# The first block of z in halves on two engines each, and the third turn moved into the tile of a pair of banks

## Chip, cores, metric

One NeuronCore of a Trainium2 chip. The metric is the device time of one execution in microseconds, taken on the slowest core, which here is the only one. The kernel before took 1192.81 us (median of three runs, 1192.8 to 1194.91). The whole change lies in the first 13 us of the program.

## The reference

```python
# batch 8, seq S 3008, d_model 256, d_qk 64, d_ff 2048; fp32 in and out
scores = (1.0 / S) * np.matmul(z, z.transpose(0, 2, 1))
attn = np.maximum(scores, 0.0) ** 2
x = u * np.matmul(attn, v)                    # [8, 3008, 256]
h = x.reshape(-1, 256) @ w_in                 # [24064, 2048]
y = (h * np.cos(h)) @ w_out                   # [24064, 256]
```

## The kernel before

It works on blocks of 512 rows of z. At the start each block of the first batch is loaded as f32, cast to f16, turned on TensorE (four transposes of 128x128) and copied from PSUM to `zT`. From `zT` come the scores, in groups of 128x1024 over two PSUM banks. Each group passes through a relu into a tile `r` and a square into a tile `A`, and `A` is multiplied with v (the "products" below). The program order on each engine is the order of this code. Waits between engines are put in by the framework, tile by tile.

```python
turned = [ppool.tile([P, CW], FP16, name=f"turned{i}", tag=f"M{i % 2}") for i in range(3)]
turned_e = ppool.tile([P, 2, 2 * CW], FP16, name="turned_e", tag="E2")     # two banks
turned += [turned_e[:, 0, 0:CW], turned_e[:, 1, 0:CW], turned_e[:, 0, CW:2 * CW]]
...
def emit_score(later=None):
    ...                                       # two or four matmuls into e, 128x1024 f32
    r = rpool.tile([P, 2, CW], FP16, name="r")
    nc.scalar.activation(r[:, :, 0:W], e[:, :, 0:W], AF.Relu)
    def square(): ...                         # nc.vector.tensor_tensor(a4, r, r, ALU.mult)
    if later is None:
        square()
    else:
        later.append(square)
...
def copy_turned(g):
    dst = zTs[0][:, g * CW:(g + 1) * CW]
    if g == 0:
        nc.scalar.copy(dst, turned[g])
    else:
        nc.vector.tensor_copy(dst, turned[g])
...
for i in range(7):                            # warm-up
    nc.tensor.matmul(E[i % 2][:, 0, :], warm[:, 0:P], warm, start=True, stop=True)
cast_z(nc.vector, 0)
cast_z(nc.vector, 1)
cast_z(nc.vector, 2)
for g in range(3, NC):
    cast_z(nc.gpsimd, g)
    ...
squares = []
turn_on_pe(0)
copy_turned(0)
turn_on_pe(1)
copy_turned(1)
emit_score(later=squares)
emit_score(later=squares)
turn_on_pe(2)
copy_turned(2)                                # third copy, ahead of the squares
squares.pop(0)()
squares.pop(0)()
M = [ppool.tile([P, CW], FP32, name=f"M{i}", tag=f"M{i}") for i in range(2)]

def filler(n):                                # matmuls whose result nobody reads
    for i in range(n):
        nc.tensor.matmul(M[1], warm[:, 0:P], warm, start=True, stop=True)

turn_on_pe(3)
copy_turned(3)
filler(2)
emit_score()
filler(1)
emit_score()
filler(1)
...
phase_a_first(0, 12, {4: lambda: turn_late(4), 8: lambda: turn_late(5)})   # products; fifth, sixth turn
```

In the text turns, copies, scores, relus and squares are counted from one: the third turn is `turn_on_pe(2)`.

## Time and profile before

| | kernel before |
|---|---|
| median of three runs | 1192.81 us |
| span of the profiled execution | 1191.2 us |
| TensorE busy, and its share of the chain that ended last | 99%, 98% |
| first score starts | 5.46 us |
| third score, first product, sixth score start | 7.41, 8.75, 12.15 us |

The sixth score is a convenient milestone: from the first products on, both kernels have the same instructions in the same order, so a difference in its start time is the whole effect of the change on the start. The prediction below shows the stretches, the chain and VectorE's order. TensorE's own timeline shows how the turns stand in it (columns: start, busy time, engine, source line, operation, output from inputs, shapes, count, and in brackets the idle time ahead with what ended it):

```profile
6.43 0.40 PE L658 MATMUL turned<-id,z 128*128 128x128 f16 x4
6.66 0.39 PE L658 MATMUL turned_e<-id,z 128*128 128x128 f16 x4
6.88 0.59 PE L696 MATMUL M<-s 128*128 128x512 f16 x2
7.41 0.39 PE L202 MATMUL E<-zT 64*128 64x512 f16 x2
```

The fourth turn (`turned_e`, 6.66) follows the third (`turned`, 6.43) at once, because it has a tile of its own. Two fillers (L696) bridge the time until the third score.

### The profile page before, as it was taken

What the parts mean: (1) busy time and instruction counts of PE and PEld (TensorE: products, weight loads), DVE (VectorE), ACT (ScalarE), POOL (GpSimd) and SP (SyncE); (2) the same over time, 40 slices, a digit from 0 to 9 for tenths busy, and PEclk for the clock granted to TensorE, in tenths of its full rate; (3) what the DMA queues carried; (4) which work ended last, traced back from release to release, by engine and by line L of the source; (5) the groups of instructions that cost most, each with busy time, mean ns of one, the idle gap of its engine ahead of it and who ended that gap; (6) DMA issues with size and microseconds to landing.
All of it is one profiled execution on the core that took longest, in us unless ns stands there. A gap on an engine that the chain in (4) does not pass through costs nothing.

```text
span 1191.2 us, 29044 instructions
## 1 busy us (share of the span) xinstructions
PE 1183.7 (99%) x11887; PEld 726.8 (61%) x11887; DVE 1011.5 (85%) x1302; ACT 794.9 (67%) x927; POOL 679.0 (57%) x717
## 2 busy tenths in 40 slices
PE   9999999999999999999999999999999999999998
PEld 4556665665566656666566665656666566665566
DVE  6888888889988898888988889888888888888776
ACT  7966676667666676667676676666766666666454
POOL 3286745657466573755647556476555655545452
PEclk9999999999999999999999999999999999999999
DMA  9999999569995799955999469984798837974301
GB/s 160 175 172 158 115 171 130 102 122 104 173 127 101 123 137 166 126 89 103 155 152 130 86 106 158 168 123 70 120 162 152 122 72 120 173 122 84 65 20 54
DMA packets 449142, 148.00 MB, mean 124 GB/s; under 512 B 401264, under 2 KB 432496, under 8 KB 449008
## 3 DMA queue, kind: packets, MB, share of 16 engines
q1 hardware_dynamic: 368464, 112.93, 56.6%
q0 software_dynamic: 80032, 32.78, 27.7%
q8 instruction: 93, 1.52, 0.5%
q10 hardware_dynamic: 512, 0.43, 0.1%
q14 instruction: 41, 0.34, 0.1%
HBM read 66.32 MB, written 24.64 MB: 76 GB/s over the span
## 4 chain that ended last, share of the span: by engine, by line
PE 98%; ACT 1%; DVE 1%; issue 0%; POOL 0%; DVEq 0%; ACTq 0%
PE E L412 27%; PE M L490 23%; PE M L266 20%; PE E L266 19%; PE E L202 6%; PE M L533 1%; ACT r L212 1%; PE M L468 1%; DVE g L423 0%; PE E L673 0%; DVE sm L278 0%; PE E L533 0%; POOL s L441 0%; PE M L696 0%; ACT c L420 0%
## 5 line engine op out<-in xcount | busy, mean ns | idle before, releaser
L420 ACT ACTIVATE c<-E 128x1024 f16<-128x1024 f32 (+1 forms) x384 | 385.7, 1007 | 216.4 <-PE E L412 214.1
L423 DVE SCALAR_TENSOR_TENSOR g<-E,c 128x1024 f16<-128x1024 f32 (+1 forms) x384 | 458.9, 1197 | 62.0 <-ACT c L420 60.9
L212 ACT ACTIVATE r<-E 128x512 f16<-128x512 f32 (+1 forms) x342 | 328.0, 967 | 112.3 <-PE E L202 106.6
L266 PEld LDWEIGHTS <-v 64*128 64x128 f16 x4512 | 245.7, 94 | 229.6 <-issue 18.8
L412 PE MATMUL E<-x,w_in 128*128 128x512 f16 (+1 forms) x1408 | 354.0, 375 | 0.0
L441 POOL TENSOR_TENSOR s<-g 128x512 f16<-128x512 f16 (+1 forms) x184 | 207.8, 1130 | 189.3 <-DVE g L423 139.4
L266 PE MATMUL M<-A,v 64*128 64x512 f16 (+1 forms) x2256 | 283.0, 372 | 0.0
L266 PE MATMUL E<-A,v 64*128 64x512 f16 (+1 forms) x2256 | 278.0, 371 | 0.0
L442 POOL TENSOR_TENSOR g<-g 128x512 f16<-128x512 f16 (+1 forms) x184 | 219.0, 1190 | 14.4
L412 PEld LDWEIGHTS <-w_in 128*128 128x128 f16 x1536 | 133.1, 98 | 108.9 <-issue 19.5
L490 PEld LDWEIGHTS <-g 128*128 128x128 f16 x2816 | 172.5, 98 | 40.8
L217 DVE TENSOR_TENSOR A<-r 128x1024 f16<-128x1024 f16 x240 | 173.2, 734 | 15.1 <-ACT r L212 14.3
L294 POOL TENSOR_TENSOR x<-sm,uT 128x512 f16<-128x512 f32 (+1 forms) x43 | 48.6, 1131 | 223.5 <-DVE sm L278 223.5
L490 PEld LDWEIGHTS <-s 128*128 128x128 f16 x2112 | 129.4, 98 | 32.1 <-DVE s L448 0.5
L202 PE MATMUL E<-zT 64*128 64x512 f16 (+4 forms) x684 | 128.0, 356 | 1.6 <-DVE sm L278 0.7
L448 DVE TENSOR_TENSOR s<-s,g 128x1024 f16<-128x1024 f16 (+1 forms) x92 | 99.7, 1085 | 2.1 <-POOL s L441 2.1
L490 PE MATMUL M<-w_mix,s 128*128 128x128 f16 x1408 | 94.0, 219 | 0.3 <-POOL s L441 0.3
L490 PE MATMUL M<-w_mix,g 128*128 128x128 f16 x1408 | 93.6, 219 | 0.0
L490 PE MATMUL M<-w_out,g 128*128 128x128 f16 x1408 | 93.6, 219 | 0.0
L220 DVE TENSOR_TENSOR A<-r 128x512 f16<-128x512 f16 (+1 forms) x102 | 80.1, 785 | 8.6 <-ACT r L212 7.6
L202 PEld LDWEIGHTS <-zT 64*128 64x128 f16 x684 | 38.7, 94 | 38.4 <-issue 3.8
L450 DVE TENSOR_TENSOR s<-g,s 128x1024 f16<-128x1024 f16 (+1 forms) x92 | 60.6, 661 | 0.0
(58 smaller groups left out, 636.3 us busy)
## 6 DMA issues: line engine op xcount, KB each, us to landing
out_dram<-o SPq DMA_DIRECT2D x87, 256.0 KB, 2.1
v<-in_v_dram POOLq DMA_DIRECT2D x40, 256.0 KB, 11.5
u<-in_u_dram POOLq DMA_DIRECT2D x40, 256.0 KB, 4.5
A<-A SPq DMA_TRANSPOSE x252, 5.3
z<-in_z_dram POOLq DMA_DIRECT2D x14, 192.0 KB, 10.9
z<-in_z_dram POOLq DMA_DIRECT2D x14, 176.0 KB, 6.8
v<-in_v_dram POOLq DMA_DIRECT2D x8, 192.0 KB, 16.1
u<-in_u_dram POOLq DMA_DIRECT2D x8, 192.0 KB, 3.7
```

The lines of the kernel that those rows point to most:

```text
L202: nc.tensor.matmul(e[:, t, 0:Wt], zT[rows, k * P:(k + 1) * P], zT[rows, J * CW:J * CW + Wt], start=True, stop=True,)
L212: nc.scalar.activation(r[:, :, 0:W], e[:, :, 0:W], AF.Relu)
L217: nc.vector.tensor_tensor(a4, r4, r4, ALU.mult)
L220: nc.vector.tensor_tensor(a4, r[:, :, 0:W], r[:, :, 0:W], ALU.mult)
L266: nc.tensor.matmul(bank[:, 0:width(J)], vs[b, k // 4][t * H:(t + 1) * H, k % 4, dh * P:(dh + 1) * P], value_rhs(b, J, k, t), start=start, ...
L412: nc.tensor.matmul(e[:, f, 0:W], w_in16[:, k, ft * P:(ft + 1) * P], x[:, k, 0:W], start=(k == 0), stop=(k == 1),)
L420: nc.scalar.activation(c[:, :, 0:W], e[:, :, 0:W], AF.Sin, bias=half_pi, scale=inv_s2)
L423: return lambda: nc.vector.scalar_tensor_tensor(gs[m][:, 2 * i:2 * i + 2, 0:W], e[:, :, 0:W], 1.0, c[:, :, 0:W], ALU.mult, ALU.mult)
L441: nc.gpsimd.tensor_tensor(s1[:, f, 0:n], g[:, f, low], g[:, lower, low], ALU.add)
L442: nc.gpsimd.tensor_tensor(g[:, f, low], g[:, f, up], g[:, f, low], ALU.subtract)
L448: nc.vector.tensor_tensor(s2[:, f, 0:n], s1[:, f, 0:n], g[:, f, up], ALU.subtract)
L490: nc.tensor.matmul(acc[:, k * P:(k + 1) * P], left[:, ft, k * P:(k + 1) * P], right[:, ft, :], start=(ft == 0 and k == 0), stop=(ft == F - ...
```

## The change

Its intent, as far as the code tells it: shorten the way to the first scores by splitting the cast, the copy and the relu of the first block over two engines each; free the bank M0 by moving the third turn into the pair of banks; and start the first two squares before the third copy.

```diff
@@ -73,9 +73,12 @@
     mark = kpool.tile([1, 2], FP16, name="mark")
     z32_all = gpool.tile([P, NC, 4, dqk], FP32, name="z32", tag="g")
     z32 = [z32_all[:, i, :, :] for i in range(NC)]
-    turned = [ppool.tile([P, CW], FP16, name=f"turned{i}", tag=f"M{i % 2}") for i in range(3)]
+    turned = [ppool.tile([P, CW], FP16, name=f"turned{i}", tag=f"M{i}") for i in range(2)]
     turned_e = ppool.tile([P, 2, 2 * CW], FP16, name="turned_e", tag="E2")
-    turned += [turned_e[:, 0, 0:CW], turned_e[:, 1, 0:CW], turned_e[:, 0, CW:2 * CW]]
+    turned += [
+        turned_e[:, 1, 0:CW], turned_e[:, 0, 0:CW],
+        turned_e[:, 1, CW:2 * CW], turned_e[:, 0, CW:2 * CW],
+    ]
     E = [ppool.tile([P, 2, CW], FP32, name=f"E{i}", tag=f"E{i}") for i in range(2)]
 
     ctx.enter_context(tc.manual_schedule())
@@ -187,7 +190,7 @@
     turn_slots = {}
     done_groups = [0]
 
-    def emit_score(later=None):
+    def emit_score(later=None, shared=False):
         b, J, I, h = groups[done_groups[0]]
         done_groups[0] += 1
         cut = I == J and not (b == 0 and J < 3)
@@ -209,7 +212,11 @@
         key = (b, J, I)
         a = new_piece(key) if h == 0 else piece(key)
         r = rpool.tile([P, 2, CW], FP16, name="r")
-        nc.scalar.activation(r[:, :, 0:W], e[:, :, 0:W], AF.Relu)
+        if shared:
+            nc.scalar.activation(r[:, 0, 0:W], e[:, 0, 0:W], AF.Relu)
+            nc.vector.tensor_scalar_max(r[:, 1, 0:W], e[:, 1, 0:W], 0.0)
+        else:
+            nc.scalar.activation(r[:, :, 0:W], e[:, :, 0:W], AF.Relu)
         def square():
             if I > J:
                 a4 = a.rearrange("p (k t j) -> p t k j", k=4, j=P)[:, 2 * h:2 * h + 2, :, :]
@@ -649,21 +656,22 @@
     make_identity(nc, id16)
     load_v(0, 0)
 
-    def cast_z(eng, g):
-        dst = z16s[0][:, 4 * g:4 * g + 4, :].rearrange("p k (t d) -> p k t d", t=2)
-        eng.tensor_copy(dst, z32[g].unsqueeze(2).to_broadcast([P, 4, 2, dqk]))
+    def cast_z(eng, g, lo=0, hi=4):
+        dst = z16s[0][:, 4 * g + lo:4 * g + hi, :].rearrange("p k (t d) -> p k t d", t=2)
+        eng.tensor_copy(dst, z32[g][:, lo:hi, :].unsqueeze(2).to_broadcast([P, hi - lo, 2, dqk]))
 
     def turn_on_pe(g):
         for k in range(4):
             nc.tensor.matmul(
                 turned[g][:, k * P:(k + 1) * P], z16s[0][:, 4 * g + k, :], id16,
-                is_transpose=True, start=(k == 0 and g < 5), stop=(k == 3),
+                is_transpose=True, start=(k == 0 and g < 4), stop=(k == 3),
             )
 
     def copy_turned(g):
         dst = zTs[0][:, g * CW:(g + 1) * CW]
         if g == 0:
-            nc.scalar.copy(dst, turned[g])
+            nc.vector.tensor_copy(dst[:, 0:T], turned[g][:, 0:T])
+            nc.scalar.copy(dst[:, T:CW], turned[g][:, T:CW])
         else:
             nc.vector.tensor_copy(dst, turned[g])
 
@@ -671,22 +679,21 @@
     nc.scalar.activation(wc[:, 0, 0:P], warm[:, 0:P], AF.Sin)
     for i in range(7):
         nc.tensor.matmul(E[i % 2][:, 0, :], warm[:, 0:P], warm, start=True, stop=True)
-    cast_z(nc.vector, 0)
+    cast_z(nc.vector, 0, 0, 2)
+    cast_z(nc.gpsimd, 0, 2, 4)
     cast_z(nc.vector, 1)
+    turn_on_pe(0)
+    copy_turned(0)
     cast_z(nc.vector, 2)
     for g in range(3, NC):
         cast_z(nc.gpsimd, g)
         if g == 3:
             load_v(0, 1)
     squares = []
-    turn_on_pe(0)
-    copy_turned(0)
     turn_on_pe(1)
     copy_turned(1)
+    emit_score(later=squares, shared=True)
     emit_score(later=squares)
-    emit_score(later=squares)
-    turn_on_pe(2)
-    copy_turned(2)
     squares.pop(0)()
     squares.pop(0)()
     M = [ppool.tile([P, CW], FP32, name=f"M{i}", tag=f"M{i}") for i in range(2)]
@@ -695,11 +702,13 @@
         for i in range(n):
             nc.tensor.matmul(M[1], warm[:, 0:P], warm, start=True, stop=True)
 
+    turn_on_pe(2)
+    copy_turned(2)
+    filler(1)
     turn_on_pe(3)
+    emit_score()
     copy_turned(3)
     filler(2)
-    emit_score()
-    filler(1)
     emit_score()
     filler(1)
 
```

## The prediction

> **What bounds it now.** I read the page's busy times first, then the whole chain of waits by line, then a table of stretches, then the chain and the timeline of the first 13 us, because the change touches nothing later than that.
>
> ```profile
> PE 1183.7 (99%) x11887; PEld 726.8 (61%) x11887; DVE 1011.5 (85%) x1302; ACT 794.9 (67%) x927; POOL 679.0 (57%) x717
> ...
> PE 98%; ACT 1%; DVE 1%; issue 0%; POOL 0%; DVEq 0%; ACTq 0%
> ...
> 8.75:12.57 3.82, 3.63 (x33) 1.50 (x34) 2.97 (x7) 2.16 (x3) 3.82 (x6) 1.00 0.62 71
> 12.57:24.00 11.43, 11.43 (x108) 5.95 (x106) 7.92 (x13) 11.42 (x14) 1.95 (x4) 1.00 1.22 194
> ...
> 60.00:1191.00 1131.00, 1126.55 (x11434) 697.61 (x11432) 967.46 (x1236) 743.48 (x870) 661.90 (x688) 1.00 0.84 122
> ```
>
> TensorE is 98% of the chain and busy 1126.55 of the last 1131 us. From 12.57 to 24.00 TensorE and ScalarE are both busy all the time (11.43 and 11.42 of 11.43 us). So nothing behind 12.57 us can take up a shift of the start: whatever the start gains or loses goes to the end one to one. Even a start of no length would save about 1%. The question is therefore one of a few tenths of a us up to two or three.
>
> The start, from the chain in order of time and the timeline:
>
> ```profile
> 4.36 0.44 PE turned L658 x4
> 4.82 0.59 ACT zT L666
> 5.46 1.03 PE E L202 x2
> 6.49 0.33 PE turned L658 x4
> 6.83 0.22 PE turned_e L658 x4
> ...
> 8.82 0.97 PE M L266 x8
> 9.79 0.33 PE turned_e L658 x4
> ...
> 12.15 0.41 PE E L202 x2
> ```
> ```profile
> 3.48 1.10 DVE L654 CAST z<-z 128x512 f16<-128x512 f32 x3 [2.35 <-DMA z<-in_z_dram]
> 6.86 0.42 DVE L668 COPY zT<-turned 128x512 f16<-128x512 f16 x1 [1.19 <-PE turned L658]
> 7.20 1.57 DVE L220 TENSOR_TENSOR A<-r 128x1024 f16<-128x1024 f16 x2
> 8.69 0.42 DVE L668 COPY zT<-turned_e 128x512 f16<-128x512 f16 x1
> 9.03 1.58 DVE L217 TENSOR_TENSOR A<-r 128x1024 f16<-128x1024 f16 x2
> ```
>
> The reader should see the order on VectorE: the third copy (6.86) stands ahead of the first two squares (7.20), and the fourth (8.69) ahead of the third and fourth squares (9.03). TensorE walks through turns, scores, fillers and the first products almost without a gap from 6.43 to 12.15.
>
> **The Trainium skill.** "PSUM — Partial Sum Buffer", PSUM bank collisions raise a hardware error: two engines may not touch one bank (in the same 32 partitions) at once, reads against reads included, so readers have to be kept apart. The trace before agrees only in that no bank there is read by two engines at once; the waits of the changed program show the consequence below. "SBUF — State Buffer", Who interferes with whom: VectorE in a two-port mode, or with two SBUF inputs against a GpSimd instruction that reads SBUF, shuts GpSimd out, or the other way round. The trace agrees in kind: GpSimd's casts took 0.61 us, but the one that met two squares 0.89. "ScalarE: Activation LUTs", What ACT_TABLE_LOAD costs: an ACTIVATE has a fixed part plus 0.833 ns an element; the trace has 1024 elements at 1.02 us and 512 at 0.59, the same slope. "TensorE: Matmul & The Clock Gate", Part 1: an idle window of about 3.4 us halves TensorE's clock. No such case is in this trace after its warm-up (turns start 107 ns apart at 4.15, 56 ns apart from 6.49).
>
> **The change part by part**, with the order and the waits of the built changed program at hand. They are the same as before from the first products on, except for what follows. Costs of halves are estimates from the rows. ScalarE: 1.02 for 1024 and 0.59 for 512, so 0.37 for 256. VectorE: 0.69 for a square of 1024 and 0.42 for a copy of 512, both f16, so 0.29 for 256; a 512-element read of f32 out of PSUM took 0.68 (sm<-M). Signals cost 0.04 to 0.07 us in the records (turn ends 4.784, copy starts 4.821; relu ends 7.138, square starts 7.204).
>
> Cast in halves: the whole cast ran 3.48 to 3.91, but TensorE's seven warm-up matmuls start 0.427 us apart, 3.723 being the last, so the first turn can't start before 4.15, as it did. The faster cast is worth 0. GpSimd's half waits for the same landing (3.456) and takes, as an estimate, 0.4 us; if VectorE's two casts shut it out until 4.1, two of the four turns come at 4.55, some 0.2 late. I count 0.05.
>
> Copy in halves: both halves lie in one bank, and in the built program ScalarE's half waits for VectorE's half, not for the turn. So 4.82 + 0.29 + 0.04 + 0.37 = 5.52, where the whole copy ended at 5.41. Loss 0.11.
>
> Relu in halves: VectorE's half waits for ScalarE's half. ScalarE's runs from 6.11 + 0.11 = 6.22 to 6.82, VectorE's from 6.89 (0.07 for the signal) to 7.57. r is whole at 7.57 in place of 7.14; the first square goes from 7.20 to about 7.62 and ends at 8.31, the second runs to 8.92 (before: 8.78). ScalarE itself is free 0.3 us sooner, for the second relu.
>
> Third turn into the pair of banks, and the new order: this is the large term. The squares now come before the third copy on VectorE, and the third copy runs at about 8.84 to 9.26 in place of 6.86 to 7.29. The fourth turn now shares a tile with the third, and in the built program it waits for the third copy; before it followed the third turn at once, at 6.66. TensorE, in order, has one filler between and then stands from about 7.2 to 9.31. Behind the fourth turn is the third score. A turn and the gap behind it take 0.33 (11.233 to 11.563 in the records), so that score starts at 9.64 in place of 7.41: 2.2 us late.
>
> From there: third relu 10.06 to 11.09 (7.94 to 8.97 before); filler, filler, fourth score, filler, at 0.216 each, and the first eight products from about 10.8 (before 8.75) to 11.7. The fifth turn waits for the fourth copy, which now stands behind the third square: 11.09 + 0.07 + 0.69, then 0.42 less 0.08 of overlap, so 12.19; the turn starts at 12.24 in place of 9.72. TensorE stands another 0.55 us. After it the order is as before: fifth score 0.77 behind that turn, sixth score 2.43 behind it, so 14.67 in place of 12.15.
>
> Sum at the sixth score: +2.5 by this walk. Of it 2.2 is the wait of the fourth turn and 0.3 that of the fifth, the copy's 0.11 and the relu's part being within the first. Before, there were 0.19 us of wait ahead of the sixth score that need not all return, and the walk takes no credit for ScalarE's earlier second relu. I take 2.3. From 12.57 on the order and work are those of before, with TensorE full, so 1192.8 + 2.3 = 1195.1.
>
> **Rivals.** First, the one that the change was made for: casts, copy and relu each in half the time, first score some 0.4 us sooner, third copy not waited for, and 1192.4 or less. For it speaks that the chain runs through the ScalarE copy (0.59) and relu (1.02 each) at the start; against it the waits of the built program, which put the halves one behind the other. Second, the late turns are absorbed: ScalarE gains 0.3 us on the second relu, products could run ahead, and the stretch to 24 us hides the rest; the time stays at 1192.8 to 1193.3. Against it: in 12.57 to 24.00 TensorE is full, 11.43 of 11.43, as is ScalarE, and only 0.19 us of wait stands ahead of 12.15. Third, the two us of standstill let TensorE's clock fall back, and the scores and products from 9.3 to some 13 us run at half speed: about 3 us of TensorE work there would add up to 3 us, giving 1197 to 1198. Against it: the standstill is shorter than the window of that page and has filler work on both sides. Fourth, GpSimd is shut out of its half cast for longer and every step moves by 0.2 to 0.5: 1195.3 to 1195.6.
>
> **Range and chances.** The kernel before ran at 1192.8 twice and 1194.9 once, so single runs scatter by 2 us. The second rival sets the low end, 1193.5, the third the high end, 1197.2. Two per cent is 24 us, as long as the whole start: within 2% is all but certain. I think it slower by some 0.2%, with about one chance in ten that it is not slower at all.
>
> **What would show it.** Right: the half copies of block 0 stand in line (ScalarE's starting about 5.15), likewise the half relus; VectorE's order is copy, half relu, two squares, third copy at about 8.8; a standstill of TensorE of about 2 us before the fourth turn, put down to the copy of zT on VectorE, and a second of about half a us before the fifth; the sixth score near 14.6; from there equal durations, and the span 2 to 2.5 us longer. Wrong: the fourth turn starting before 8.5; the third copy ahead of the squares; TensorE full from 7 to 12 us; or the shift at 14.6 us not found again at the end.

## The result, and the profile after

The changed kernel took 1197.38 us (median of 6 runs, 1196.83 to 1197.96). The kernel before took 1193.18 (6 runs, the three above among them, 1192.8 to 1197.65). The ratio of fast runs is 1.0028 with a 95% interval of 1.0013 to 1.0043: slower, and well within 2%. All runs were fast, that is, none was over 1.5% above the fastest of its kernel. Here and below a ratio is the mean time of one kernel's fast runs over that of the other's fast runs of the same rounds, so it is not quite the ratio of the medians quoted. The profiled spans are 1191.2 and 1195.3, so 4.1 us longer.

The direction was as predicted, and so was the wait. The size was not: 2.3 us were predicted, 4.1 came, because TensorE's clock, which the prediction had put aside, and a held-up square came on top. Against the 1192.81 known at the time, the ratio gives 1196.1, inside the range (the one long execution of before, 1197.65, makes the ratio smaller); the median of the runs lies 0.2 us above its upper end.

The stretches of the changed kernel (columns: stretch and length in us, then busy us and count for PE, PEld (weight loads), DVE, ACT, POOL, then TensorE's granted clock, DMA share, GB/s; a clock of 1.00 is full, 0.50 half. The column shows 1.00 also ahead of the first clock record, here at 6.14 us, although the turns at 4.15 still start 107 ns apart):

```profile
4.15:8.75 4.60, 2.47 (x18) 1.35 (x17) 2.95 (x7) 1.88 (x3) 3.05 (x5) 1.00 1.01 135
8.75:12.57 3.82, 2.91 (x11) 0.76 (x10) 1.55 (x4) 1.20 (x2) 3.82 (x6) 0.60 0.76 90
12.57:16.00 3.43, 3.43 (x29) 1.30 (x29) 1.70 (x5) 1.84 (x2) 1.43 (x3) 0.94 1.32 163
```

From 8.75 to 12.57 TensorE did 11 matmuls where it had done 33, and its clock column fell from 1.00 to 0.60. That column is the surprise. The chain of the changed kernel in order of time (start, length, engine, what):

```profile
4.82 0.30 DVE zT L673
...
5.14 0.38 ACT zT L674
...
6.21 0.60 ACT r L216
...
6.84 0.70 DVE r L217
...
7.57 1.71 DVE A L227 x2
9.28 0.34 DVE zT L676
...
9.66 0.58 PE turned_e L665 x4
10.25 0.54 PE E L205 x2
10.79 0.96 PE M L703 x2
```

The halves stand one behind the other, as predicted: VectorE's half copy, then ScalarE's; ScalarE's half relu, then VectorE's. Then come both squares, the third copy, and only then the fourth turn. The timeline of the same stretch:

```profile
6.37 0.40 PE L665 MATMUL turned_e<-id,z 128*128 128x128 f16 x4
6.60 0.38 PE L703 MATMUL M<-s 128*128 128x512 f16 x1
...
7.57 1.71 DVE L227 TENSOR_TENSOR A<-r 128x1024 f16<-128x1024 f16 x2
7.64 1.09 POOL L661 CAST z<-z 128x512 f16<-128x512 f32 x1 [1.23 <-DMA z<-in_z_dram]
...
9.66 0.58 PE L665 MATMUL turned_e<-id,z 128*128 128x128 f16 x4 [2.69 <-DVE zT L676]
```

Three things are to be seen. TensorE stands idle for 2.69 us ahead of the fourth turn, put down to the copy of `zT` on VectorE. The two squares took 1.71 us: single records give 0.69 for the first (7.57 to 8.26) and 1.10 for the second (8.18 to 9.28), beside a GpSimd cast of 1.09 (7.64 to 8.73). And the four transposes of the fourth turn took 0.58, where the four of the third took 0.40: TensorE is at half clock. In the single records the clock is low from 9.55 to 12.96 us, 3.41 us in all; the stretches agree, (1 - 0.60) x 2 x 3.82 + (1 - 0.94) x 2 x 3.43 being 3.5.

| start, us | before | predicted | after |
|---|---|---|---|
| first score | 5.46 | 5.57 | 5.57 |
| ScalarE's half copy | - | 5.15 | 5.14 |
| VectorE's half relu | - | 6.89 | 6.84 |
| first square | 7.20 | 7.62 | 7.57 |
| third copy | 6.86 | 8.84 | 9.20 |
| fourth turn | 6.66 | 9.31 | 9.66 |
| third score | 7.41 | 9.64 | 10.18 |
| first product | 8.75 | 10.8 | 12.77 |
| fifth turn | 9.72 | 12.24 | 13.81 |
| sixth score | 12.15 | 14.67 | 16.24 |

The sixth score is 4.09 us late, and ScalarE's instructions, matched one by one with those of before, stay 4.01 to 4.10 late from the fifth relu to the end (the span: +4.12). What had to be found out is how the 4.09 splits.

### The profile page after: what moved, and what is told of

The parts are those of the page before. It is cut to its first block, busy times and chain, and to the rows that moved or that the text cites. A ratio compares the mean times of both kernels' runs of the same rounds, so it can differ in the third digit from the quotient of the medians.

```text
span 1195.3 us, 29046 instructions
## 1 busy us (share of the span) xinstructions
PE 1185.0 (99%) x11887; PEld 727.1 (61%) x11887; DVE 1012.5 (85%) x1304; ACT 793.9 (66%) x927; POOL 678.5 (57%) x718
## 4 chain that ended last, share of the span: by engine, by line
PE 97%; DVE 1%; ACT 1%; issue 0%; POOL 0%; DVEq 0%; ACTq 0%
PE E L419 27%; PE M L497 23%; PE M L273 20%; PE E L273 19%; PE E L205 5%; PE M L540 1%; ACT r L219 1%; PE M L475 1%; DVE g L430 0%; PE E L681 0%; DVE A L227 0%; DVE sm L285 0%; PE E L540 0%; PE M L703 0%; PE turned_e L665 0%
## 5 line engine op out<-in xcount | busy, mean ns | idle before, releaser
L219 ACT ACTIVATE r<-E 128x1024 f16<-128x1024 f32 x341 | 327.1, 966 | 116.0 <-PE E L205 110.1
L449 POOL TENSOR_TENSOR g<-g 128x512 f16<-128x512 f16 (+1 forms) x184 | 218.7, 1188 | 14.4
## 6 DMA issues: line engine op xcount, KB each, us to landing
v<-in_v_dram POOLq DMA_DIRECT2D x8, 192.0 KB, 16.2
```

What stands on the lines that cost most here:

```text
L449: nc.gpsimd.tensor_tensor(g[:, f, low], g[:, f, up], g[:, f, low], ALU.subtract)
```

## The experiments

Theory A: the shared tile and the place of the third copy behind both squares make the wait, and the wait alone is worth about 2.4 us; the rest is TensorE's clock. Rival B: the rest is VectorE being held up by GpSimd. Rival C: the halves cost more than their 0.1 us. Rival D: part of the 4.09 is something later, unrelated to the start.

All ten kernels gave correct results. The readings rest on the traces of the start. These agree closely (the first score starts at 5.57 in all nine kernels with the halves) and differ by some tenths of a us where a load of z lands earlier or later. Each median stands beside that of the kernel before on the same chip in the last columns. "Stands" is TensorE's idle time ahead of the fourth turn; "shift" is the sixth score against 12.15.

| kernel | fourth turn | stands | clock low, us | sixth score | shift | median / before | ratio |
|---|---|---|---|---|---|---|---|
| after | 9.66 | 2.69 | 3.41 | 16.24 | +4.09 | 1197.38 / 1193.18 | 1.0028 |
| own_bank | 7.15 | 0 | 0 | 13.07 | +0.92 | 1193.96 / 1193.79 | 1.0004 |
| copy_first | 7.92 | 0.8 | 0 | 13.22 | +1.07 | 1194.48 / 1193.79 | 1.0000 |
| more_filler | 9.74 | 0 | 0 | 15.04 | +2.89 | 1195.95 / 1193.79 | 1.0018 |
| pair_only | 9.04 | 2.43 | 6.83 | 17.06 | +4.91 | 1198.02 / 1193.79 | 1.0030 |
| halves | 6.34 | 0 | 0 | 12.29 | +0.14 | 1193.21 / 1193.19 | 1.0003 |
| filler_act | 9.15 | 0 | 0 | 14.45 | +2.30 | 1195.65 / 1193.19 | 1.0024 |
| vec_copy6 | 6.10 | 0 | 0 | 11.79 | -0.36 | 1194.03 / 1193.19 | 1.0006 |
| act_cast | 9.03 | 2.31 | 6.83 | 16.89 | +4.74 | 1197.70 / 1193.78 | 1.0030 |
| filler10 | 9.67 | 0.64 | 0 | 14.97 | +2.82 | 1196.47 / 1193.78 | 1.0016 |
| filler5 | 9.26 | 1.41 | 0 | 14.56 | +2.41 | 1195.56 / 1193.78 | 1.0010 |

### own_bank: the third turn back in a tile of its own

From the changed kernel; the order and the halves stay.

```diff
     turned_e = ppool.tile([P, 2, 2 * CW], FP16, name="turned_e", tag="E2")
+    turned.append(ppool.tile([P, CW], FP16, name="turned2", tag="M0"))
     turned += [
-        turned_e[:, 1, 0:CW], turned_e[:, 0, 0:CW],
-        turned_e[:, 1, CW:2 * CW], turned_e[:, 0, CW:2 * CW],
+        turned_e[:, 0, 0:CW],
+        turned_e[:, 1, 0:CW], turned_e[:, 0, CW:2 * CW],
     ]
...
-                is_transpose=True, start=(k == 0 and g < 4), stop=(k == 3),
+                is_transpose=True, start=(k == 0 and g < 5), stop=(k == 3),
...
-    M = [ppool.tile([P, CW], FP32, name=f"M{i}", tag=f"M{i}") for i in range(2)]
+    M = [None, ppool.tile([P, CW], FP32, name="M1", tag="M1")]
...
     copy_turned(2)
+    M[0] = ppool.tile([P, CW], FP32, name="M0", tag="M0")
     filler(1)
```

> The changed kernel with one thing undone: the third turn has its own tile in the bank that the first turn leaves, so the fourth turn no longer waits for the third copy; the halves and the new order (squares ahead of the third copy) stay. Theory (the shared pair makes the fourth turn wait for a copy that stands behind both squares): no standstill of TensorE before the fourth turn, third score at 7.6 us (10.18 changed, 7.41 before), granted clock full from 7 us on. The first product now waits for the third copy (it takes over that bank) at about 9.6, so the sixth score comes at about 13.1 us (12.15 before, 16.24 changed): span +0.9 us against before. Rival 1 (the halves carry the loss): sixth score stays near 16. Rival 2 (the clock falls for a reason of its own, not because of the standstill): clock 0.6 between 9 and 12.6 us again.

```profile
7.15 0.39 PE L666 MATMUL turned_e<-id,z 128*128 128x128 f16 x4
...
7.66 1.08 POOL L662 CAST z<-z 128x512 f16<-128x512 f32 x1 [0.78 <-DMA z<-in_z_dram]
9.20 0.41 DVE L677 COPY zT<-turned 128x512 f16<-128x512 f16 x1
...
9.67 0.39 PE L274 MATMUL M<-A,v 64*128 64x512 f16 x2 [0.50 <-DVE zT L677]
```

The third copy is as late as in the changed kernel (9.20), yet the fourth turn starts at 7.15. So it was the shared tile that bound the two. The same late copy now holds back the first product instead, whose bank M0 the third turn had used, but only by 0.50 us. The sixth score is 0.92 late (expected at 13.1, came at 13.07), and the end is 0.93 late. The two turns lie in different banks in the changed kernel too; the wait belongs to the tile, not to the bank.

### copy_first: the third turn and copy back ahead of the squares

From the changed kernel; the shared tile stays.

```diff
     emit_score(later=squares)
+    turn_on_pe(2)
+    copy_turned(2)
     squares.pop(0)()
     squares.pop(0)()
...
-    turn_on_pe(2)
-    copy_turned(2)
     filler(1)
```

> The changed kernel with the third turn and its copy put ahead of the two squares again; shared pair and halves stay. Theory: the third copy runs right behind the half relu, 7.45 to 7.87, the fourth turn starts at 7.92 (9.66 changed), third score 8.25. The fourth copy still stands behind the third square, so the fifth turn comes at about 10.9 (9.72 before, 13.81 changed) and the sixth score at about 13.3: span +1.2 us against before, granted clock full. Rival 1 (halves): sixth score near 16. Rival 3 (sharing the tile costs by itself, whatever the order): fourth turn not before 9.

```profile
7.46 0.41 DVE L676 COPY zT<-turned_e 128x512 f16<-128x512 f16 x1
...
7.92 0.38 PE L665 MATMUL turned_e<-id,z 128*128 128x128 f16 x4 [0.82 <-DVE zT L676]
```

The third copy runs at 7.46, behind VectorE's half relu and ahead of the squares, and the fourth turn waits 0.8 us for it. The sixth score is 1.07 late (13.3 expected, 13.22 came), at full clock. So each of the two parts, the shared tile and the place of the copy, takes the large wait away when undone. The span was 2.0 longer, not the 1.2 expected. The other 0.9 us appears at 56.6 us:

```profile
56.59 1.05 PE L540 MATMUL M<-w_out,g 128*128 128x256 f16 x8 [0.74 <-DMA w_out<-in_moe_w_out_dram]
```

There the first products with w_out wait for its load, which took 16.4 us from issue to landing, against 14.4 in the trace of before. This is rival D in kind: a later wait that some executions have. It also came in pair_only (+1.03), filler10 (+0.7) and act_cast (+0.3), and one of +1.1 near 98 us in more_filler. In the changed kernel's own trace nothing of the sort happened, since the shift is 4.09 at the sixth score and 4.12 at the end.

### pair_only: the pair of banks and the new order, without any halves

From the kernel before: the third turn into `turned_e` and the order of the changed kernel; cast, copy and relu whole as before.

```diff
-    turned = [ppool.tile([P, CW], FP16, name=f"turned{i}", tag=f"M{i % 2}") for i in range(3)]
+    turned = [ppool.tile([P, CW], FP16, name=f"turned{i}", tag=f"M{i % 2}") for i in range(2)]
...
-    turned += [turned_e[:, 0, 0:CW], turned_e[:, 1, 0:CW], turned_e[:, 0, CW:2 * CW]]
+    turned += [
+        turned_e[:, 1, 0:CW], turned_e[:, 0, 0:CW],
+        turned_e[:, 1, CW:2 * CW], turned_e[:, 0, CW:2 * CW],
+    ]
...
-    turn_on_pe(2)
-    copy_turned(2)
     squares.pop(0)()
     squares.pop(0)()
...
+    turn_on_pe(2)
+    copy_turned(2)
+    filler(1)
     turn_on_pe(3)
+    emit_score()
     copy_turned(3)
     filler(2)
     emit_score()
     filler(1)
-    emit_score()
-    filler(1)
```

> The kernel before with only the third turn into the pair of banks and the new order; cast, copy and relu whole. Theory (this part alone makes the loss): first square 7.20, second to about 8.8 (or 9.1 where GpSimd's cast holds it), third copy to 9.1 to 9.5, fourth turn at 9.2 to 9.6 (6.66 before), and a standstill of 2.0 to 2.5 us; if the clock falls as in the changed kernel, sixth score at 15.7 to 16.2 and span +3.6 to +4.1; if it does not, sixth score at about 14.4 and span +2.3. Rival 1 (halves carry it): sixth score near 12.2, span as before.

```profile
8.75:12.57 3.82, 3.53 (x15) 0.92 (x16) 1.27 (x3) 1.87 (x2) 3.82 (x6) 0.50 0.62 70
12.57:16.00 3.43, 3.43 (x22) 1.15 (x18) 1.12 (x2) 0.34 (x2) 2.03 (x4) 0.58 1.27 156
```

Every wait came 0.6 us sooner than in the changed kernel (fourth turn 9.04, a standstill of 2.43), yet the sixth score was later, at 17.06 and not 15.7 to 16.2. The clock column says why: 0.50 and 0.58, low for 6.83 us, twice the 3.41 of the changed kernel. My expectation had counted one such stretch. So the pair of banks and the order are enough for the slowdown; the halves are not needed for it. They do lengthen the wait in this order, though: VectorE's half relu stands ahead of the squares, and the second square starts at 8.18 us with it in the changed kernel, at 7.87 without it here.

### halves: the three halves alone

From the kernel before: the casts, copies and the relu of the changed kernel; tiles and order of the turns as before.

```diff
-    cast_z(nc.vector, 0)
+    cast_z(nc.vector, 0, 0, 2)
+    cast_z(nc.gpsimd, 0, 2, 4)
     cast_z(nc.vector, 1)
+    turn_on_pe(0)
+    copy_turned(0)
     cast_z(nc.vector, 2)
...
-            nc.scalar.copy(dst, turned[g])
+            nc.vector.tensor_copy(dst[:, 0:T], turned[g][:, 0:T])
+            nc.scalar.copy(dst[:, T:CW], turned[g][:, T:CW])
...
-    emit_score(later=squares)
+    emit_score(later=squares, shared=True)
     emit_score(later=squares)
```

(`emit_score` and `cast_z` with the parameters of the changed kernel.)

> The kernel before with the three halved operations alone (cast, copy and relu of block 0); banks and order as before. Theory: the halves of the copy and of the relu stand in line, so the first score starts at 5.57 (5.46 before), the first r is whole at 7.54 (7.14 before), third score at 7.6 (7.41), and most of it is lost in waits that were there anyway: sixth score at 12.2 to 12.5 us (12.15 before), span +0.1 to +0.3 us. Rival 1 (the halves carry the loss): several us. Rival 4 (the halves gain, as intended, and only the bank spoils it): sixth score before 12.1.

The sixth score came at 12.29, 0.14 late; the time is unchanged (ratio 1.0003, 0.9991 to 1.0016). So in the old order the halves cost 0.14 us. In the new order they delay the squares by some 0.3 us (pair_only, above); that is a part of the wait. Rival C is right for this much and no more. The reason for the change is gone too: both halves of the copy together end 0.11 us later than the whole copy, because ScalarE's half waits for VectorE's:

```profile
5.15 0.37 ACT L671 COPY zT<-turned 128x256 f16<-128x256 f16 x1 [1.41 <-DVE zT L670]
```

### more_filler and filler_act: the same wait with TensorE kept busy

More fillers ahead of the fourth turn keep TensorE busy while it would stand. In filler_act the last of GpSimd's casts of z also goes to ScalarE, so that nothing runs beside the second square.

```diff
     copy_turned(2)
-    filler(1)
+    filler(13)
     turn_on_pe(3)
```

```diff
-    for g in range(3, NC):
+    for g in range(3, NC - 1):
         cast_z(nc.gpsimd, g)
...
     emit_score(later=squares)
+    cast_z_act(NC - 1)              # nc.scalar.copy of the same operands
     squares.pop(0)()
```

> The changed kernel with 13 fillers in place of one ahead of the fourth turn, so that TensorE is busy (with work for nothing) for the time it stood still; every wait stays. Theory (the standstill lets the clock fall, and the low clock costs about 1.4 us on top of the wait): clock full throughout 8.75 to 16 us (0.60 and 0.94 changed), fourth turn still at 9.66, third score at 10.0, sixth score at about 14.8 (16.24 changed, 12.15 before): span about +2.7 us against before in place of +4.1. Rival (the clock is not what costs): sixth score at 16.2 with a full clock.

> The kernel with 13 fillers, and with the last cast of z moved from GpSimd to ScalarE, which stood idle from 7.7 to 10.8 us, so that no GpSimd cast runs beside the second square. Theory (the second square took 1.10 in place of 0.69 us[...]): second square 0.69 us, third copy 8.8 to 9.2, fourth turn at 9.27 (9.66 with fillers alone), sixth score about 0.4 earlier than with fillers alone, near 14.4. Rival (the second square was slow for another reason): 1.10 us again.

In more_filler the clock stayed at 1.00, but thirteen fillers were too many: they ran to 9.74 and held the fourth turn themselves, 0.5 us beyond the third copy's end (9.20). Its shift of 2.89 is therefore an upper bound. The fillers were as long in filler_act, but TensorE had come to them sooner, and its shift was 2.30, with 0.69 for the second square. Both say that without the clock's fall the wait costs between 2.3 and 2.9, and both leave about 1.2 us or more to the clock. The number of fillers had to be set better.

### filler10 and filler5: the standstill cut to 0.6 and to 1.4 us

The edit of more_filler with 10 and with 5 in place of 13.

> The changed kernel with 10 fillers in place of one ahead of the fourth turn (13 had held the fourth turn back themselves, to 9.74 where the copy was done at 9.20). Theory: clock full; the fourth turn follows the third copy at 9.2 to 9.7, according to whether GpSimd's cast holds the second square; sixth score at 14.4 to 14.9 (16.24 changed), span +2.3 to +2.8 against before unless a later transfer adds a wait. Rival (the clock is not what costs): 16.2.

> The changed kernel with 5 fillers: TensorE stands still for 1.2 to 2.0 us instead of 2.7. Neither theory says from which length on the clock falls here (at 0.8 us it stayed full, at 2.7 and 2.4 it fell). If it stays full: sixth score at 14.4 to 14.9; if it falls: 15.5 to 16.3.

filler10 turned out to be the changed kernel in every respect of the start but the clock and the nine more fillers: its third copy starts at 9.21 and its fourth turn at 9.67 (after: 9.20, 9.66), and the second square took 1.10 us there too.

```profile
7.58 1.71 DVE L227 TENSOR_TENSOR A<-r 128x1024 f16<-128x1024 f16 x2
...
9.67 0.38 PE L665 MATMUL turned_e<-id,z 128*128 128x128 f16 x4 [0.64 <-DVE zT L676]
...
11.49 1.04 PE L273 MATMUL M<-A,v 64*128 64x512 f16 x8
```

From the fourth turn to the first product both kernels have the same matmuls. Filler10 took 11.49 - 9.67 = 1.82 us for them, the changed kernel 12.77 - 9.66 = 3.11. The difference of 1.29 is what is found again at the sixth score, 16.24 - 14.97 = 1.27. That is the price of the clock.

In filler5 chance gave the second half of the answer. Its last block of z landed later, and GpSimd's cast came at 8.20, just behind the start of the second square (8.18). In the changed kernel it came during the first square, and so had its turn ahead of the second:

```profile
7.58 1.29 DVE L227 TENSOR_TENSOR A<-r 128x1024 f16<-128x1024 f16 x2
...
9.26 0.38 PE L665 MATMUL turned_e<-id,z 128*128 128x128 f16 x4 [1.41 <-DVE zT L676]
```
```profile
8.20 1.14 POOL L661 CAST z<-z 128x512 f16<-128x512 f32 x1 [0.73 <-DMA z<-in_z_dram]
```

The two squares together took 1.29, the third copy began at 8.79, the cast was the one held up (1.14 us). TensorE stood for 1.41 us and kept its clock. The sixth score is 2.41 late, and 2.45 are found at the end. So filler5 is the wait by itself, filler10 the wait and the held-up square (2.82 - 2.41 = 0.41, the 1.10 - 0.69 of the square), and the changed kernel both and the clock: 2.41 + 0.41 + 1.27 = 4.09. As a sum of differences it has to close; what supports it is that the square's own duration gives the 0.41 and the stretch from the fourth turn to the first product the 1.29. Rival B is right for a tenth of the shift.

### act_cast: no cast beside the square, and the standstill left in

filler_act with one filler again, that is the changed kernel with the last cast on ScalarE.

```diff
-    filler(13)
+    filler(1)
```

> As the run with fillers and the cast on ScalarE, but with one filler again, as in the changed kernel: so it differs from the changed kernel only in the last cast (no GpSimd work beside the second square), and from the filler run only in that TensorE stands still. Theory: second square 0.69 us, third copy 8.6 to 9.0, fourth turn at about 9.0, then a clock below full until 12 us or later; sixth score 1.2 to 1.6 us later than with fillers (14.45), so at about 15.8, span +3.6 against before. Rival (the clock costs nothing, the fillers were only in the way): sixth score at 14.4 or earlier.

```profile
8.75:12.57 3.82, 3.54 (x15) 0.92 (x16) 1.26 (x3) 1.83 (x2) 2.87 (x5) 0.50 1.23 147
12.57:16.00 3.43, 3.43 (x23) 1.12 (x20) 1.12 (x2) 0.56 (x2) 0.00 (x0) 0.63 1.36 196
```

The second square took 0.68 us and the fourth turn came 0.63 sooner than in the changed kernel, as theory and rival had both said. The end was not sooner: the clock was low for 6.83 us, and the sixth score came at 16.89, not near 15.8. Against filler_act, which differs in the fillers alone, the clock cost 2.44 us, nearly twice the 1.27. So the clock costs about 1.25 us for each stretch of 3.41, and an edit that shortens the wait can still lose by drawing two stretches.

### vec_copy6: can the start be made shorter at all?

From the kernel before: the first copy whole on VectorE, and one warm-up matmul fewer.

```diff
-        if g == 0:
-            nc.scalar.copy(dst, turned[g])
-        else:
-            nc.vector.tensor_copy(dst, turned[g])
+        nc.vector.tensor_copy(dst, turned[g])
...
-    for i in range(7):
+    for i in range(6):
```

> The kernel before with what the change seems to have wanted, got in another way: block 0 copied whole by VectorE (0.42 us) in place of ScalarE (0.59), and six warm-up matmuls in place of seven, so that the first turn starts at 3.96, right behind the cast, and not at 4.15. If the start is a plain chain: first score at 5.1 (5.46), sixth score at 11.8 (12.15), span -0.35 us. Rival: the later steps are held by something else (the casts on GpSimd, the landings of z) or the clock rises later with one matmul less; then the sixth score stays at 12.1 or later.

```profile
5.17 0.77 PE L202 MATMUL E<-zT 64*128 64x512 f16 x4
```

The first score came 0.29 us sooner and the sixth 0.36 sooner, at 11.79 as expected. The gain lasted to 36 us. There a relu on ScalarE ends at 36.32 and the next copy of a sum starts at 36.55, where it started before; the profile names no releaser for the gap. From there on ScalarE's instructions start when they did before, from 56 us on 0.2 us later, and from 589 us on 0.5 us later. In device time nothing was gained (ratio 1.0006, 0.9994 to 1.0019). The two edits were not tried apart. No version tried beats the kernel before.

## Why the prediction was right or wrong

**Halves worth nothing: right.** The half copies and half relus stand in line in the built program and on the chip, to within 0.05 us of the times predicted. "The faster cast is worth 0" held: the first turn started at 4.15 in both. The 0.05 us set aside for VectorE's casts shutting GpSimd out was not seen; GpSimd's half took 0.51 and was done at 3.99, and it was VectorE's second cast that took 0.62 in place of 0.42, with no consequence. The halves alone cost 0.14 us; in the new order they delay the squares by some 0.3 us, close to the walk (first square 7.62 predicted, 7.57 measured). Which shared tile puts the halves in line, the one they read or the one they write, was not tested.

**The wait of the fourth turn: right, and right in size.** In filler5, where neither of the two other terms acts, the fourth turn starts at 9.26 (predicted 9.31), the fifth at 12.14 (12.24), the sixth score at 14.56 (14.67), a shift of 2.41 where the prediction's sum gave 2.5 and I took 2.3.

**The standstill before the fifth turn: its time was right, its length not.** The walk (the prediction's sum step by step) gave fillers and scores 0.216 us each, but between matmuls of different kinds the starts are 0.32 apart, so the products began at 11.08 in filler5 and not at 10.8. They took up the 0.55 us but for 0.1. In the changed kernel slow products hid the rest.

**The second square: mis-sized.** It "runs to 8.92", I wrote, at the 0.69 of an undisturbed square. GpSimd's cast ran beside it, and it ended at 9.28. That is 0.41 us of the 4.09. I had seen such a meeting in the trace of before (a cast at 0.89 in place of 0.61), but only as a cost to GpSimd.

**The clock: the step that failed.** The third rival was this very thing, and I put it aside with "the standstill is shorter than the window of that page and has filler work on both sides". The standstills of 2.3 to 2.7 us halved the clock in all three kernels that have them; those of 1.4 us and less did not. In the timed runs it is the same: the mean granted clock is 0.997 to 0.999 in all six of the changed kernel and 0.997 or 0.998 in all twelve of pair_only and act_cast, and 0.999 or 1.000 in all twenty of the four kernels with more fillers. For the changed kernel alone this would be thin: own_bank and the kernel before have 0.998 too, each in one long execution (1199.74 and 1198.02 us), and the mean also takes in the half clock of the last 1 to 4 us of every trace. The sum had no term for it; it is 1.27 us. The rival's own estimate was up to 3 us, for scores and products at half speed over all of that stretch. It was less because the stretch ended after 3.41 us, and because the gaps of some 0.1 us between unlike matmuls do not lengthen: a score with the gap behind it took 0.32 us in filler10 and 0.54 in the changed kernel, so 0.22 more and not 0.32.

**"Nothing behind 12.57 us can take up a shift": right for the changed kernel** (4.09 at the sixth score, 4.12 at the end), and for own_bank, filler_act and filler5 to within 0.04. It isn't a law: vec_copy6 lost its 0.36 us at 36 us, and some executions gained about 1 us at the load of w_out. With such events, and a scatter of before from 1192.66 to 1198.02, the device times separate the kernels only in groups: ratios of 1.0028 to 1.0030 for the three with a low clock, 1.0010 to 1.0024 for the four with more fillers, 1.0000 to 1.0006 for the rest.

**What stays open.** Why the low clock lasted one stretch in the changed kernel and two in pair_only and act_cast was not tested. Whether the square or the cast is held up depends on when the last block of z lands in each execution; the split of the 4.09 is that of the profiled execution.

## What to carry to other kernels

Here the framework tied two uses of one tile together although they lie in different banks: the next writer waited for the last reader of another part. So ask where that reader stands in its engine's queue before a buffer is merged or an order is changed. Splitting an instruction over two engines gains nothing where the halves share the tile that orders them; look in the built program for what the second half waits for. And give a new standstill of TensorE two terms, the wait itself and a stretch at half clock behind it: here 2.4 us of wait drew another 1.3 to 2.4 us, which matmuls that nobody reads could prevent.

## What the Trainium skill lacked or had wrong

- "TensorE: Matmul & The Clock Gate", Part 1, in its table of the two states, lays the return to half clock to an idle window of about 3.4 us. Here standstills of 2.69, 2.43 and 2.31 us were enough; 1.41, 0.8 and 0.64 were not. The page's window length of 3413 ns agrees: the low stretches lasted 3.41 us in the changed kernel and 6.83 us in the two others. A reading that fits all of these, untested: what counts is the busy share of each whole stretch of 3.41 us. TensorE was busy for about 25%, 34% and 40% of the one before the fall (6.14 to 9.55 us in the changed kernel, 5.23 to 8.65 in pair_only, 4.89 to 8.30 in act_cast), and filler5 can't have been below 59% in any; the clock stayed low after stretches that were 88% and 79% busy, and rose after one of 97%. The page gives no such shares.
- "SBUF — State Buffer", Who interferes with whom, agrees with most of these meetings: the one that comes second waits for all of the other. In filler10 the first square ended at 8.27, the cast that came at 7.97 ended 0.47 us after that, and the second square 0.54 us after the cast; in filler5 the cast ended 0.47 us after the second square. More_filler does not fit so plainly: there the cast had come at 8.16, 0.02 ahead of the second square and 0.10 before the first one's end, and yet it ended 0.47 after the second. What the page lacks is the time that a square and a cast lose in such a meeting: 0.41 us for the square of 128x1024, 0.53 for the cast of 128x512 (1.14 in place of 0.61).
- No page looked at gives the cost of halving a cast on GpSimd: 128x256 took 0.51 us, 128x512 took 0.61.
- "PSUM — Partial Sum Buffer", PSUM bank collisions raise a hardware error, gives its rule by bank and quadrant. The wait that cost most here followed the tile: third and fourth turn were in different banks, and the fourth waited 2.69 us with one tile and not at all with two. No page has this.
